# Two shared pools of on-chip buffers in a mixed attention kernel, with the order planned anew

## The chip, the cores and the metric

The kernel runs on one core of one Trainium2 chip. A core has five engines that run side by side, each through its own list of instructions: TensorE (PE, matmuls; PEld is its loading of weights), VectorE (DVE), ScalarE (ACT, here the exponentials), GpSimd (POOL) and SyncE (SP, which here issues nearly all DMAs). They wait for each other by semaphores. The metric is the device time of one launch in microseconds.

## The reference

The input x has 2048 rows of 512 numbers. Two attentions with 32 heads of 16 numbers each work on the same x, and a gate per row mixes them.

```python
x = A_x
g = _sigmoid((x * gate_w).sum(-1, keepdims=True))
a = _A_ref(x, A_wqkv, A_w_phi, A_wo)     # linear attention
b = _B_ref(x, B_wqkv, B_wo)              # full softmax attention
return g * a + (1 - g) * b

# in A, with q, k, v of x @ wqkv per head:
pq = einsum("bhsd,hdf->bhsf", q, w_phi)
phi_q = concatenate([softmax(pq), softmax(-pq)])      # the same for k
kv = einsum("bhsf,bhsd->bhfd", phi_k, v)
z  = einsum("bhsf->bhf", phi_k)
o  = einsum(phi_q, kv) / (einsum(phi_q, z) + 1e-6)     # then @ wo

# in B:
p = softmax(einsum("bhqd,bhkd->bhqk", q, k) * 0.25)
o = einsum("bhqk,bhkd->bhqd", p, v)                    # then @ wo
```

B is the great part of the work: 32 heads of 2048 x 2048 scores, each with an exponential.

## The kernel before

**Work of B.** It is cut into 32 sets. A set has 512 queries (a quarter), a group of 8 heads of which it takes 4, and all 2048 keys as 16 key tiles of 128. For a key tile PE makes the scores of the four heads (L1249, into the seven banks of psR, keys in the partitions and 512 queries along the row), an engine takes exponentials, and PE adds the products with the values into psO (L1300). The exponential of a key tile runs in one of two ways. On ACT it is the exponential function, two instructions of 128 x 1024, each into a buffer of the ring E (L1264). On DVE it is four instructions of 128 x 512 that write 16-bit integers, whose bits are read as a rough bf16 exponential, into a buffer of the ring T (L1269); two copies of it with a small constant added, in two buffers of the ring TS, correct it. Such a shift is one instruction of DVE (L1281) or of POOL (L1284), and the products with these copies use values scaled beforehand (vS). Six of the 16 key tiles of a set may go either way; the rest is for ACT. At the end of a set psO is copied out (OT), turned by a DMA transpose (OTT), divided by its sums (ob, L1211) and, for every pair of sets, turned again into oBT (L1330).

**Work of A.** The maps' weights are first multiplied into the projection: WAT, the turned weights of A, times a block matrix of w_phi gives Wp (L1018). For every 128 rows, `phi` makes one full matmul of x and Wp, two exponentials on ACT (L1077), and the sums of 16 neighbours on POOL in steps: L1083 into a buffer `tr`, L1088, L1089, then L1092 or L1093; POOL then scales the map (L1096 for queries, L1099 for keys). Key maps stay in the ring phk until the 4 tiles of a quarter are multiplied with the values vA (L1122). Query maps are turned by DMA into phT (L1153), multiplied with kz (L1159), divided and gated into oA (L1165), and turned by DMA into oAT (L1169). The gate itself is 64 matmuls of one column in four groups of 16 (L1001), and one matmul of four columns for a certificate on the size of gate_w (L1047). The last projections (L1346, L1358) read oAT and oBT, and 16 tiles of 128 x 512 go out (L1372, L1375).

**Buffers.** In the kernel before each kind has its own ring: 12 of E, 6 of phk, 3 of T, 4 of TS, 2 each of oAT and oBT. xT, W_Av, WAT and Wp are tensors of their own. When weights are no longer needed, their room is used again: the query maps and `tr` lie in WAT, phT and the last outputs in half of Wp, oA and the other outputs in W_Av.

**Order.** The order of each engine's list is made when the program is built, by a planner (`_Sched`). Every operation has an engine, a due time, a length and a delay until its result is there; a DMA transpose has for instance 1.3 us of issue and 2.0 or 2.6 us until it has landed. The planner goes through time and places on each engine the ready operation that can start first, with due times to settle ties, and its own rules for PE (`_pick_pe`) and for which of two ways a key tile takes. An operation that needs a buffer gets one that is free by the planner's times, among several the one with the highest number:

```python
got = sorted(times, key=lambda i: (max(times[i], when), -i))[:len(ts)]
```

The new owner then depends on all operations of the old one (`advance`), and `plan` turns the dependencies that are not implied by others into semaphore waits. The table `STYLES` gives a seed for each stretch of `WINDOW` us of planned time; the seed sets the tolerances of the planner's choices in that stretch (0 stands for the fixed ones).

**The other way out.** A flag computed on the chip says whether the score sizes allow these shortcuts; if not, the same program runs a plain version (`_general`) afterwards. With the inputs given it is skipped.

Of the kernel before, what the change touches and what calls it, by code (L numbers as in the profile page):

```python
# [14 lines left out]
D = 512  # L15
H = 32
DH = 16
# [27 lines left out]
NE_, NPH = 12, 6  # L45
WINDOW = 3.0
STYLES = (
# [478 lines left out]
def _general(fast):  # L526
# [9 lines left out]

    xT, Wp, W_Av, WAT, kz, kvs = ns.xT, ns.Wp, ns.W_Av, ns.WAT, ns.kz, ns.kvs
    T = [x.bitcast(BF16) for x in ns.T_r.aps + ns.TS_r.aps]
# [10 lines left out]
    qst_r, qz_r, oAT_r, oBT_r = sub(ns.qst_r), sub(ns.qz_r), sub(ns.oAT_r), sub(ns.oBT_r)  # L549
# [7 lines left out]
    wat = add("sp", lambda e: e.dma_start_transpose(WAT[:], ns.A_wqkv[:, 0:2 * D]), dma=True)  # L557
    wav = add("sp", lambda e: e.dma_start(W_Av[:], ns.A_wqkv.rearrange("(t p) c -> p t c", p=128)[:, :, 2 * D:3 * D]), dma=True)
    ewp = []
    for w in range(2):  # L560
        for t in range(KT):
            m = _Tile(M_r)

            def fn(e, m=m, w=w, t=t):
                ins = None
                for r in range(KT):
                    ins = e.matmul(m.ap[:, 128 * r:128 * (r + 1)], lhsT=WAT[:, 4 * w + r, 128 * t:128 * (t + 1)],
                                   rhs=ns.Wbd[:, r, :], start=True, stop=True)
                return ins
            f = add("pe", fn, [wat], [m])  # L570
            ewp.append(add("dve", lambda e, m=m, w=w, t=t: e.tensor_copy(Wp[:, w, t, :], m.ap), [f], [m]))
# [9 lines left out]
    def phi(w, st, out):  # L581
        m, mx, d, ee, ss = _Tile(M_r), _Tile(st_r), _Tile(d_r), _Tile(e_r), _Tile(ss_r)
        f = project(m, lambda t: xT[:, t, 128 * st:128 * (st + 1)], lambda t: Wp[:, w, t, :], ewp)
# [16 lines left out]
    for qd in range(4):  # L600
        items = []
        for st in range(4 * qd, 4 * qd + 4):
            ph, va, m = _Tile(phk_r), _Tile(vA_r), _Tile(M_r)
            o = phi(1, st, ph)
            f = project(m, lambda t, st=st: xT[:, t, 128 * st:128 * (st + 1)], lambda t: W_Av[:, t, :], [wav])
# [25 lines left out]
    for qc in range(QC):  # L631
# [32 lines left out]
        for g in range(KT):  # L664
            m, qs, qz = _Tile(M_r), _Tile(qst_r), _Tile(qz_r)
            f = project(m, lambda t, g=g: ns.W_Bq[:, t, 128 * g:128 * (g + 1)], lambda t, qc=qc: xT[:, t, NQ * qc:NQ * (qc + 1)], [])
# [57 lines left out]
def _build(ctx, nc, A_x, A_wqkv, A_w_phi, A_wo, B_wqkv, B_wo, gate_w, out):  # L724
# [58 lines left out]
    wp1 = Wp[:, 1].rearrange("p a b -> p (a b)")  # L783
# [360 lines left out]
    for st in range(NT):  # L1144
# [4 lines left out]
        if st % 4 == 0:  # L1149
            oat[st // 4] = _Tile(oAT_r)  # L1150
# [330 lines left out]
```

## Time and profile before

| | |
|---|---|
| device time, three runs | 697.72, 698.08, 700.85 us; median 698.08 us |
| the profiled execution | 696.97 us |
| span in its profile, first to last instruction | 695.1 us |
| mean granted clock of TensorE in it | 0.990 |
| busy: PE, DVE, ACT, POOL | 656.6, 656.6, 661.1, 525.5 us |

The page of the profile gives busy times, a chain of work followed back from the last instruction, and groups of instructions: line, engine, operation, what is written and read, shapes and type, count, then the busy time in us and the mean time of one in ns, then the idle time of the engine just before them and what ended most of it. A busy time of ACT or DVE is that of the union: neighbours overlap, so one instruction can last longer than the pace at which they follow each other. SPq and ACTq are the queues in which an engine issues DMAs. The granted clock is the share of full speed that TensorE was given. A tile is named by the tensor that it lies in, without its number: "WAT" in a row of POOL is a query map or a `tr` buffer.

### The profile page before, as it was taken

What the parts mean: (1) busy time and instruction counts of PE and PEld (TensorE: products, weight loads), DVE (VectorE), ACT (ScalarE), POOL (GpSimd) and SP (SyncE); (2) the same over time, 40 slices, a digit from 0 to 9 for tenths busy, and PEclk for the clock granted to TensorE, in tenths of its full rate; (3) what the DMA queues carried; (4) which work ended last, traced back from release to release, by engine and by line L of the source; (5) the groups of instructions that cost most, each with busy time, mean ns of one, the idle gap of its engine ahead of it and who ended that gap; (6) DMA issues with size and microseconds to landing.
All of it is one profiled execution on the core that took longest, in us unless ns stands there. A gap on an engine that the chain in (4) does not pass through costs nothing.

```text
span 695.1 us, 16428 instructions
## 1 busy us (share of the span) xinstructions
PE 656.6 (94%) x6760; PEld 213.9 (31%) x6760; DVE 656.6 (94%) x1111; ACT 661.1 (95%) x747; POOL 525.5 (76%) x433
## 2 busy tenths in 40 slices
PE   8999999999999999999998999999899999999996
PEld 4343343332323223233332223232222332222221
DVE  5899979999999999999999999999999999999995
ACT  6999979999999999999999999999999999999992
POOL 6689868887687766777777787778777976777883
PEclk9999989999999999999999999999999999999998
DMA  6501000001000000001022211223221221220001
GB/s 153 152 17 14 19 2 17 16 25 29 11 17 17 9 16 9 17 16 48 16 47 39 40 40 44 47 43 60 24 40 40 52 41 40 38 41 17 16 9 34
DMA packets 72768, 23.81 MB, mean 34 GB/s; under 512 B 64624, under 2 KB 72688, under 8 KB 72688
## 3 DMA queue, kind: packets, MB, share of 16 engines
q1 hardware_dynamic: 71472, 21.93, 15.5%
q8 instruction: 54, 0.88, 0.5%
q10 hardware_dynamic: 1216, 0.79, 0.4%
q14 instruction: 26, 0.21, 0.1%
HBM read 4.21 MB, written 2.10 MB: 9 GB/s over the span
## 4 chain that ended last, share of the span: by engine, by line
ACT 63%; PE 26%; DVE 6%; POOL 2%; DMA 2%; issue 1%; POOLq 0%; DVEq 0%
ACT E L1264 59%; PE psR L1249 9%; PE psO L1300 8%; PE psR L896 4%; DVE T L1269 3%; PE psR L1346 2%; ACT WAT L1077 2%; POOL TS L1284 2%; DMA OTT<-OT 2%; PE psR L958 2%; ACT phk L1077 2%; DVE TS L1281 1%; PE psR L910 1%; DVE ob L1211 0%; DVE OT L879 0%
## 5 line engine op out<-in xcount | busy, mean ns | idle before, releaser
L1264 ACT ACTIVATE E<-psR 128x1024 bf16<-128x1024 f32 x670 | 629.5, 1105 | 14.5 <-PE psR L1249 8.0
L1269 DVE TENSOR_SCALAR T<-psR 128x512 int16<-128x512 f32 x708 | 447.3, 680 | 14.4 <-PE psR L1249 9.6
L1284 POOL TENSOR_TENSOR TS<-T,shc 128x1024 int32<-128x1024 int32 x194 | 364.3, 1891 | 55.9 <-DVE TS L1281 39.7
L1249 PE MATMUL psR<-qz,kT 32*128 32x512 bf16 (+1 forms) x2048 | 292.2, 386 | 28.1 <-ACT E L1264 21.1
L1249 PEld LDWEIGHTS psR<-qz,kT 32*128 32x128 bf16 (+1 forms) x2048 | 77.6, 91 | 274.5 <-ACT E L1264 197.3
L1300 PE MATMUL psO<-TS,vS 128*18 128x512 bf16 x1416 | 125.3, 382 | 2.1 <-POOL TS L1284 1.4
L1300 PE MATMUL psO<-E,vB 128*18 128x512 bf16 x1340 | 122.2, 381 | 0.0
L1281 DVE TENSOR_SCALAR TS<-T 128x2048 int16<-128x2048 int16 x160 | 107.6, 705 | 0.5
L1300 PE MATMUL psO<-T,vB 128*18 128x512 bf16 x708 | 69.2, 381 | 0.0
L1096 POOL TENSOR_TENSOR WAT<-WAT,ss 128x1024 bf16<-128x1024 bf16 x16 | 30.9, 1929 | 26.4 <-DVE TS L1281 24.0
L1300 PEld LDWEIGHTS psO<-TS,vS 128*18 128x18 bf16 x1416 | 30.0, 88 | 57.7 <-issue 31.7
L1099 POOL TENSOR_TENSOR phk<-phk,ss 128x1024 bf16<-128x1024 bf16 x16 | 30.9, 1929 | 22.0 <-DVE TS L1281 21.1
L1300 PEld LDWEIGHTS psO<-E,vB 128*18 128x18 bf16 x1340 | 31.1, 88 | 44.3 <-issue 30.5
L896 PE MATMUL psR<-xT,WB 128*128 128x512 bf16 x128 | 33.7, 388 | 0.1
L896 PE MATMUL psR<-Wp,xT 128*128 128x512 bf16 x128 | 33.2, 382 | 0.6 <-DVE T L1269 0.4
L1083 POOL TENSOR_TENSOR WAT<-phk 128x512 f32<-128x512 bf16 x16 | 18.5, 1154 | 13.3 <-DVE TS L1281 12.6
L1083 POOL TENSOR_TENSOR WAT<-WAT 128x512 f32<-128x512 bf16 x16 | 18.5, 1155 | 12.1 <-DVE TS L1281 11.5
L1088 POOL TENSOR_TENSOR tr<-WAT 128x256 f32<-128x256 f32 x32 | 23.3, 728 | 2.3 <-DVE TS L1281 1.3
L1300 PEld LDWEIGHTS psO<-T,vB 128*18 128x18 bf16 x708 | 17.3, 88 | 20.8 <-issue 17.5
L879 DVE CAST OT<-psO 128x512 bf16<-128x512 f32 x31 | 21.1, 681 | 0.0
L1077 ACT ACTIVATE WAT<-psR 128x512 bf16<-128x512 f32 x32 | 18.9, 697 | 0.0
L1089 POOL TENSOR_TENSOR tr<-tr 128x128 f32<-128x128 f32 x32 | 12.7, 398 | 7.8 <-DVE TS L1281 7.0
(116 smaller groups left out, 362.4 us busy)
## 6 DMA issues: line engine op xcount, KB each, us to landing
qz<-qst SPq DMA_DIRECT2D x120, 16.0 KB, 1.8
out_dram<-WAv SPq DMA_DIRECT2D x12, 128.0 KB, 1.7
WB<-in_B_wqkv_dram SPq DMA_DIRECT2D x3, 384.0 KB, 5.1
T<-in_A_x_dram SPq DMA_DIRECT2D x2, 256.0 KB, 4.4
T<-in_A_x_dram ACTq DMA_DIRECT2D x2, 256.0 KB, 4.8
WAv<-in_A_wqkv_dram SPq DMA_DIRECT2D x1, 512.0 KB, 5.4
WB<-in_B_wo_dram SPq DMA_DIRECT2D x1, 512.0 KB, 3.3
WB<-in_A_wo_dram SPq DMA_DIRECT2D x1, 512.0 KB, 3.6
```

Of the source, the lines that this page charges most:

```text
L896: calls = [lambda e, t=t: e.matmul(tile.ap[:, off:off + 512], lhsT=lhs(t), rhs=rhs(t), start=(t == 0), stop=(t == KT - 1)) for t in range(KT)]
L1077: ex = [add("act", prio, 0.48, lambda e, s=s: e.activation(ev()[:, :, 16 * s:16 * s + 16], P(), ACTF.Exp, scale=1.0 - 2.0 * s), deps=[f] + ...
L1083: p1 = pool(prio + 2, 1.14, lambda e: e.tensor_tensor(v8(), eg()[:, :, 0:8], eg()[:, :, 8:16], ALU.add), ex + use_wat, tiles=[ee, tr], nam ...
L1088: p2 = pool(prio + 2, 0.72, lambda e: e.tensor_tensor(u4(), v8()[:, :, 0:4], v8()[:, :, 4:8], ALU.add), [p1], tiles=[tr, tr2])
L1096: return pool(prio + 6, 1.9, lambda e: e.tensor_tensor(eg(), eg(), ss.ap[:, 0, :].unsqueeze(2).to_broadcast([128, 64, DH]), ALU.mult), p4, ...
L1099: return pool(prio + 6, 1.9, lambda e: e.tensor_tensor(eg(), eg(), ss.ap[:, 1, :].unsqueeze(2).to_broadcast([128, 64, DH]), ALU.mult), [o7 ...
L1249: ins = e.matmul(rs[h].ap, lhsT=kT[a:a + n, g, 128 * kt:128 * (kt + 1)], rhs=qt.ap[a:a + n, c, :], start=True, stop=True, tile_position=(a ...
L1264: exps.append(add("act", pr + 0.5 * cc, 0.905, lambda e, rs=rs, E=E: e.activation(E.ap.rearrange("p (a n) -> p a n", n=512), pair(rs), ACT ...
L1269: exps.append(add("dve", pr + 0.5 * cc + 0.01 * h, 0.6, lambda e, rs=rs, T=T, cc=cc, h=h: e.tensor_scalar(T.ap[:, 1024 * cc + 512 * h:1024 ...
L1281: sh.append([add("dve", pr + 1.0 + 0.3 * m, 0.6, lambda e, T=T, X=X, m=m: e.tensor_single_scalar(X.ap, T.ap, SHIFT[m], ALU.add), deps=exps ...
L1284: sh[-1].append(pool(pr + 1.0 + 0.3 * m, SHP, lambda e, T=T, X=X, m=m: e.tensor_tensor(X.ap.bitcast(I32), T.ap.bitcast(I32), shc[:, m - 1: ...
L1300: ins = e.matmul(O.ap[32 * col:32 * col + VW, :], lhsT=lhs(hd), rhs=rhs(cc)[:, 512 * h:512 * (h + 1)], start=(first_pv[s] == key), stop=(l ...
```

## The change

Nothing of the arithmetic changes. The rings become two pools:

- E has 16 buffers of 128 x 1024 bf16 (256 KB). It holds exponentials of ACT, key maps, query maps, their turned form, `tr`, oA, output tiles and the small scratch of the certificate.
- T has 20 buffers of 128 x 2048 16-bit numbers (512 KB), one tensor. It holds the DVE tiles and both shifted copies, x as staged and the four quarters of the turned x, the two neighbouring halves of WAT, the value weights of A, the second half of Wp, and the maps oAT and oBT.

Every user takes a buffer when the planner places it and gives it back when the last reader is done; the tensors that were reused by hand are gone, and with them the waits for the last use of the old weights (`use_wat`, `use_wav`, `use_wp1`). DMAs that write or read pool buffers (phT, oAT, output) get a semaphore each instead of one per buffer. The order of all engines is planned anew, with a table of seeds for stretches of 2 us in place of 3 us. The plain version loads x again, since its buffers have been reused. Line numbers grow by 6 to 7 in the places named above (L1264 is L1270, L1088 is L1095).

```diff
-NE_, NPH = 12, 6
-WINDOW = 3.0
+NE_, NT_, NPH = 16, 20, 5
+WINDOW = 2.0
 STYLES = (
...
-    xT = sb([128, KT, S], name="xT")
-    W_Av = sb([128, KT, D], name="WAv")
-    WAT = sb([128, 8, D], name="WAT")
-    Wp = sb([128, 2, KT, D], name="Wp")
+    Wp0 = sb([128, KT, D], name="Wp")
...
     E_r = ring(NE_, [128, 1024], name="E")
-    T_r = ring(3, [128, 2048], I16, name="T")
-    TS_r = ring(4, [128, 2048], I16, name="TS")
-    phk_r = ring(NPH, [128, 1024], name="phk")
+    T_all = sb([128, NT_, 2048], I16, name="T")
+    T_r = _Slots([T_all[:, i, :] for i in range(NT_)])
+    TS_r = T_r
+    phk_r = E_r
-    oAT_r = ring(2, [128, KT, NQ], name="oAT")
-    oBT_r = ring(2, [128, KT, NQ], name="oBT")
...
-    watv = WAT[:].rearrange("p a b -> p (a b)")
-    eA_r = _Slots([watv[:, 1024 * i:1024 * (i + 1)] for i in range(2)])
-    tr_r = _Slots([watv[:, 2048 + 1024 * i:3072 + 1024 * i].bitcast(F32) for i in range(2)])
-    phT_r = _Slots([wp1[:, 1024 * i:1024 * (i + 1)].rearrange("p (g q) -> p g q", q=128) for i in range(2)])
-    oA_r = _Slots([W_Av[:, i, :] for i in range(2)])
-    fin_r = _Slots([W_Av[:, 2 + i, :] for i in range(2)])
+    quad = lambda tile: tile.ap.bitcast(BF16).rearrange("p (t n) -> p t n", n=512)
+    xt, wat, wav, wp1 = [_Tile(T_r) for _ in range(QC)], [_Tile(T_r), _Tile(T_r)], _Tile(T_r), _Tile(T_r)
+    wat[0].mate, wat[1].mate = wat[1], wat[0]
...
-    op_wav = dma("sp", -94.5, 8.0, W_Av[:], A_wqkv.rearrange("(t p) c -> p t c", p=128)[:, :, 2 * D:3 * D], deps=op_x23, name="wav")
+    op_wav = dma("sp", -94.5, 8.0, lambda: quad(wav), A_wqkv.rearrange("(t p) c -> p t c", p=128)[:, :, 2 * D:3 * D], deps=op_x23, name="wav", tiles=[wav])
...
     def phi(prio, w, st, ee, ee_deps):
-        tile, ss, tr = _Tile(M_r), _Tile(ss_r), _Tile(tr_r)
+        tile, ss, tr = _Tile(M_r), _Tile(ss_r), _Tile(E_r)
...
-        ph, ptt, rA, oA, nd = _Tile(eA_r), _Tile(phT_r), _Tile(rA_r), _Tile(oA_r), [_Tile(M_r), _Tile(M_r)]
+        ph, ptt, rA, oA, nd = _Tile(E_r), _Tile(E_r), _Tile(rA_r), _Tile(E_r), [_Tile(M_r), _Tile(M_r)]
-            oat[st // 4] = _Tile(oAT_r)
+            oat[st // 4] = _Tile(T_r)
...
-            obt[qc] = _Tile(oBT_r)
+            obt[qc] = _Tile(T_r)
...
-        fi = _Tile(fin_r) if not last else None
+        fi = _Tile(E_r)
```

More of the change, by code (lines that the diff above doesn't have):

```diff
@@ L1000, in gate_mm @@
                 for t in range(KT):
-                    ins = e.matmul(tg.ap[:, st:st + 1], lhsT=xT[:, t, 128 * st:128 * (st + 1)], rhs=gw[:, t:t + 1],
+                    ins = e.matmul(tg.ap[:, st:st + 1], lhsT=XT(t, 128 * st, 128 * (st + 1)), rhs=gw[:, t:t + 1],
                                    start=(t == 0), stop=(t == KT - 1))
             return ins
-        gops.append(add("pe", st_(GT), 0.9, gate_mm, deps=sum(op_x, []) + op_gw, tiles=[tg], mode="full", name="gate", nb=st_(GT - 0.7)))
+        gops.append(add("pe", st_(GT), 0.9, gate_mm, deps=sum(op_x, []) + op_gw, tiles=[tg] + xt, mode="full", name="gate", nb=st_(GT - 0.7)))
     op_ge = add("act", st_(GT), 0.3, lambda e: e.activation(ez[:], tg.ap[:, 0:NT], ACTF.Exp), deps=gops, tiles=[tg])
@@ L1017, in fn, with gram @@
                 for r in range(KT):
-                    ins = e.matmul(tile.ap[:, 128 * r:128 * (r + 1)], lhsT=WAT[:, 4 * w + r, 128 * t:128 * (t + 1)],
+                    ins = e.matmul(tile.ap[:, 128 * r:128 * (r + 1)], lhsT=WAT(4 * w + r, 128 * t, 128 * (t + 1)),
                                    rhs=Wbd[:, r, :], start=True, stop=True)
                 return ins
-            f = add("pe", prio, 0.3, fn, deps=[op_wat] + op_wbd, tiles=[tile], mode="full", name="wp", nb=prio - EARLY)
+            f = add("pe", prio, 0.3, fn, deps=[op_wat] + op_wbd, tiles=[tile] + wat, mode="full", name="wp", nb=prio - EARLY)
             use_wat.append(f)
-            ev_wp[w].append(evac("dve", prio, lambda w=w, t=t: Wp[:, w, t, :], lambda tile=tile: tile.ap, [f], [tile], name="wpev"))
-    def gram(prio, src, deps, name, col):
+            ev_wp[w].append(evac("dve", prio, lambda w=w, t=t: Wp(w, t), lambda tile=tile: tile.ap, [f], [tile] + [wp1] * w, name="wpev"))
+    def gram(prio, src, deps, name, col, also=()):
         m = _Tile(M_r)
@@ L1346, in _build @@
         calls = [lambda e, tile=tile, sl=sl, src=src, w=w, n=n, early=early: e.matmul(
-            tile.ap, lhsT=src.ap[:, n % 4, sl], rhs=w[:, n % 4, :], start=(n == 0), stop=(n == 7 - early))
+            tile.ap, lhsT=quad(src)[:, n % 4, sl], rhs=w[:, n % 4, :], start=(n == 0), stop=(n == 7 - early))
             for n, (src, w) in enumerate(([(oT, WoA)] * KT + [(oBt, WoB)] * KT)[:n_mm])]
-        fi = _Tile(fin_r) if not last else None
+        fi = _Tile(E_r)
         f = chain(prio, calls, MM, [op_oAT[st], op_woA, op_woB] + [x for g in range(KT - last) for x in op_oBT[qc, g]] +
-                  (tail_qk if last and not early else []), [tile, oT, oBt] + ([fi] if fi else []), "of", prio - EARLY, 1 if last else PIECE)
-        dst = (lambda fi=fi: fi.ap) if not last else (lambda i=i: finl[i])
+                  (tail_qk if last and not early else []), [tile, oT, oBt], "of", prio - EARLY, 1 if last else PIECE)
+        dst = lambda fi=fi: fi.ap[:, 0:512]
         if early:
@@ L1358, in _build @@
             f = add("pe", st_(32.0) - 20, MM, lambda e, tile=tile, oBt=oBt, sl=sl, early=early: e.matmul(
-                tile.ap, lhsT=oBt.ap[:, KT - 1, sl], rhs=WoB[:, KT - 1, :], start=early, stop=True),
+                tile.ap, lhsT=quad(oBt)[:, KT - 1, sl], rhs=WoB[:, KT - 1, :], start=early, stop=True),
                 deps=[f, op_oBT[qc, KT - 1][i // 2]], tiles=[tile, oT, oBt], mode="full", name="os")
@@ L1369, in _build @@
                 dst(), tile.ap, omg[:, st:st + 1], None, op0=ALU.mult),
[L1370 removed]
+                deps=[f, op_omg], tiles=[tile, fi], name="fin")
         if not last:
             outs.append(add("sp", prio + 1, 0.63, lambda e, dst=dst, st=st: e.dma_start(out[0, 128 * st:128 * (st + 1), :], dst()),
[L1373 removed]
+                            deps=[ev], tiles=[fi], dma=2.0, name="out"))
         else:
             outs.append(add("act" if i == 3 else "sp", prio + 1, 0.55, lambda e, dst=dst, st=st: e.dma_start(
[L1376 to L1377 removed]
+                out[0, 128 * st:128 * (st + 1), :], dst()), deps=[ev], tiles=[fi], dma=2.6, name="out"))
     op_end = add("sp", 1e9, 0.1, lambda e: None, deps=outs, name="end")
```

106 lines of the change are left out of this document (55 added, 51 removed), and 33 rows, old and new, of the table STYLES.

## The prediction

> **What bounds the kernel now.** I read the page first: the busy times, the chain and the groups.
>
> ```profile
> PE 656.6 (94%) x6760; PEld 213.9 (31%) x6760; DVE 656.6 (94%) x1111; ACT 661.1 (95%) x747; POOL 525.5 (76%) x433
> ...
> ACT 63%; PE 26%; DVE 6%; POOL 2%; DMA 2%; issue 1%; POOLq 0%; DVEq 0%
> ...
> L1264 ACT ACTIVATE E<-psR 128x1024 bf16<-128x1024 f32 x670 | 629.5, 1105 | 14.5 <-PE psR L1249 8.0
> L1269 DVE TENSOR_SCALAR T<-psR 128x512 int16<-128x512 f32 x708 | 447.3, 680 | 14.4 <-PE psR L1249 9.6
> L1284 POOL TENSOR_TENSOR TS<-T,shc 128x1024 int32<-128x1024 int32 x194 | 364.3, 1891 | 55.9 <-DVE TS L1281 39.7
> L1281 DVE TENSOR_SCALAR TS<-T 128x2048 int16<-128x2048 int16 x160 | 107.6, 705 | 0.5
> ```
>
> ACT, DVE and PE are all busy 94 to 95% of 695.1 us, and the chain lies on ACT for 63% and on PE for 26%. All idle time of ACT is 695.1 - 661.1 = 34.0 us; that, and busy time in which its instructions follow each other late (rival D), is all that an order or a pool can win on it. The table by stretches shows where it lies (columns after the length: busy us of PE, PEld, DVE, ACT, POOL, then the granted clock).
>
> ```profile
> 12.00:50.00 38.00, 36.39 (x388) 14.84 (x387) 34.06 (x56) 36.17 (x41) 28.85 (x25) 1.00 0.40 97
> 50.00:100.00 50.00, 48.80 (x568) 19.61 (x567) 45.76 (x77) 43.47 (x48) 41.22 (x30) 0.93 0.08 12
> 100.00:150.00 50.00, 49.15 (x518) 17.54 (x518) 48.41 (x79) 48.17 (x55) 42.11 (x36) 1.00 0.06 12
> 150.00:650.00 500.00, 474.98 (x4887) 146.25 (x4883) 488.26 (x829) 495.80 (x565) 377.66 (x300) 1.00 0.16 32
> 680.00:695.10 15.10, 8.54 (x52) 2.40 (x48) 6.92 (x14) 1.64 (x3) 5.07 (x3) 0.79 0.12 38
> ```
>
> From 150 to 650 us ACT is idle for only 4.2 us. From 12 to 150 us it is idle for 1.83 + 6.53 + 1.83 = 10.2 us, while PE is near full with the projections; behind 680 us it is idle for 13.5. So the places to win are the first 150 us and the tail, and the place to lose is the long middle, where any new wait of ACT goes straight to the end. The waits and the chain give the prices:
>
> ```profile
> ACT oBT L1327 <- PE psR L1320: 8.7, 1, 8.7
> ACT E L1264 <- PE psO L1300: 4.3, 3, 3.8
> PEld psO L1300 <- issue: 79.7, 340, 0.4
> PEld psO L1300 <- POOL TS L1284: 14.2, 45, 1.0
> POOL WAT L1083 <- DVE TS L1281: 24.1, 18, 2.0
> DVE T L1269 <- POOL TS L1284: 0.4, 1, 0.4
> ...
> 67.87 2.40 DVE T L1269 x4
> 181.43 1.19 PE psO L1300 x20
> 605.42 39.96 ACT E L1264 x44
> ```
>
> In the wait rows the numbers are total us, times, longest. An E buffer that PE had not read in time stopped ACT 3 times, for 4.3 us, 3.8 of them at once. From the chain: an exponential on ACT costs 39.96/44 = 0.908 us when nothing is late, one on DVE 2.40/4 = 0.60, a group of four product matmuls into psO 1.19/5 = 0.24. A turn of PE to such products shows 79.7/340 = 0.234 us of idle weight load.
>
> **The change part by part.** Counts here are those of the two built programs' instruction orders, without times.
>
> *Work.* ACT has 668 exponentials instead of 670, DVE 712 instead of 708, DVE shifts 159 instead of 160, POOL shifts 197 instead of 194, PE 8 matmuls into psO more. ACT: -2 x 0.908 = -1.8 us. DVE: 4 x 0.60 less one shift of 0.705, +1.7. POOL: 3 x 1.891 = +5.7, covered by its 695.1 - 525.5 = 169.6 us of idle. PE: 2 groups x 0.24 = +0.5. Over ACT and DVE together the sum is about zero, so the moved tiles alone are no gain; their worth depends on which engine ends last, priced at the tail.
>
> *Turns of PE.* Changes between the three kinds of matmul (32- or 64-row scores, 18-column products, full ones) fall from 1132 to 1112. At 0.234 each that is 4.7 us, less the 0.5 above 4.2; the bounds are 0 (the idle was a wait for another engine) and 4.2. PE carries 26% of the chain, so I take 4.2 x 0.26 = -1.1.
>
> *The stop at 95 to 100 us.* The timeline there:
>
> ```profile
> 94.36 0.61 PE L1249 MATMUL psR<-qz,kT 32*128 32x512 bf16 x3
> 94.90 1.89 PE L958 MATMUL psR<-WB,xT 128*128 128x128 bf16 x16
> 95.01 1.02 ACT L1264 ACTIVATE E<-psR 128x1024 bf16<-128x1024 f32 x1 [0.81 <-PE psR L1249]
> 96.58 0.29 PE L1047 MATMUL psR<-gw,ones 128*128 128x1 bf16 x4
> 96.73 1.75 PE L896 MATMUL psR<-xT,WB 128*128 128x512 bf16 x4
> 98.42 0.40 PE L1249 MATMUL psR<-qz,kT 32*128 32x512 bf16 x4
> 99.83 1.02 ACT L1264 ACTIVATE E<-psR 128x1024 bf16<-128x1024 f32 x1 [3.80 <-PE psO L1300]
> ...
> 92.00:96.00 4.00, 4.00 (x56) 2.62 (x55) 2.52 (x6) 3.19 (x5) 1.89 (x1) 0.50 0.02 4
> 96.00:100.00 4.00, 4.00 (x42) 1.73 (x40) 2.24 (x5) 0.20 (x2) 1.41 (x3) 0.72 0.00 0
> ```
>
> After the four gate groups of 16 one-column matmuls the granted clock is 0.50, and PE takes 98.42 - 94.36 = 4.06 us from one bundle of scores to the next (a V projection, the sum of gw2, a K projection). ACT, whose 12 E buffers are full, also needs the products behind them. In the new order the same four gate groups stand together, but behind them come 6 scores, 16 products, 3 scores, V projection and sum, 5 scores. So the longest gap without scores is 1.89 + 0.29 = 2.18 us at the same low clock. Gain 4.06 - 2.18 = 1.9 us; bounds 0 (the clock stays low for longer) and 0.81 + 3.80 = 4.6 (all of it goes). I take -1.9, the row being of the same work at the same clock.
>
> *Tail.*
>
> ```profile
> 662.95 16.72 ACT L1264 ACTIVATE E<-psR 128x1024 bf16<-128x1024 f32 x18
> 679.46 2.48 DVE L1269 TENSOR_SCALAR T<-psR 128x512 int16<-128x512 f32 x4
> 682.05 1.67 DVE L1281 TENSOR_SCALAR TS<-T 128x2048 int16<-128x2048 int16 x1
> 683.80 1.89 POOL L1284 TENSOR_TENSOR TS<-T,shc 128x1024 int32<-128x1024 int32 x1 [0.63 <-DVE TS L1281]
> 685.75 0.40 PE L1300 MATMUL psO<-TS,vS 128*18 128x512 bf16 x4 [0.51 <-POOL TS L1284]
> ```
>
> ACT's last exponential ends at 679.67; the last DVE tile and its shifts hold the final product until 685.75, 6.1 us later, and ACT sits idle for the 8.7 us of the wait row. In the old order the five product groups behind the last scores are all of DVE tiles. In the new one ten groups follow, four of them of E, and the last but one is an E group: the two engines end together. With the same total work both then end at the middle of 679.67 and 685.75: -3.0 us. Bounds: 0 (they end together because ACT came later) and -6.1.
>
> *Pools.* E, phk, tr, phT, oA, fin and the exponentialed maps share 16 buffers of 256 KB (before 12 + 6, with the rest in dead weights); T, TS, input, weights and output maps share 20 of 512 KB, 4 of them held by the input for most of the run. The slack is not what the counts suggest: exponentials of ACT that must wait for a product's read are 26 before and 21 after, of DVE 29 and 34, so the planner uses the room up to the edge again. DVE tiles that wait for a POOL shift's buffer fall from 72 to 22; the row above shows that this cost 0.4 us: gain at most 0.4, taken as 0.
>
> *New waits.* 45 exponentials of ACT now wait for something that is neither PE nor ACT: 21 for POOL (the second step of a sum, L1088 before, which sets a tr buffer free), 24 for a DMA's landing (12 oAT, 8 output, 4 phT). Behind a waiting exponential stands everything else of ACT, then PE's scores, which wait for its psR banks. The DMAs:
>
> ```profile
> oAT<-WAv SPq DMA_TRANSPOSE x16, 2.4
> out_dram<-WAv SPq DMA_DIRECT2D x12, 128.0 KB, 1.7
> Wp<-WAT SPq DMA_TRANSPOSE x16, 3.2
> WAT<-in_A_wqkv_dram SPq DMA_TRANSPOSE x1, 6.0
> ...
> 23.41 3.85 SPq L834 DMA_TRANSPOSE WAT<-in_A_wqkv_dram  x1
> ...
> L1018 PE MATMUL psR<-Wbd,WAT x32: 219/220/315, 61.1 to 94.1; 128*128 128x128 bf16 x32
> ```
>
> The planner's own entries allow 1.3 + 2.0 = 3.3 us for oAT, 2.63 for an output, 3.9 for phT; the rows (2.4, 1.7, 3.2) are shorter, so I take 0 for these 24; if a queue ahead on SP made each late by as much as the margin plus 0.5 us, 12 us. For POOL there is no such margin: PE waits for POOL's shifts 184 times after and 183 before, and 45 of those before cost 14.2/45 = 0.32 us. At that rate 21 x 45/183 = 5 waits cost 0.32: +1.6 us; bounds 0 and 21 x 1.0 (the longest) = 21. Separate wait instructions rise on ACT from 1 to 47 and fall on DVE from 124 to 70; DVE keeps its 0.60 pace with 124 of them, so 0. On SP the load of A's value weights now waits for a POOL shift and a product before it goes out; behind it stand the WAT transpose and then the q spreads. WAT landed at 23.4 + 6.0 = 29.4 us and is first read at 61.1, so 31 us of lateness are covered there. The q spreads behind it feed the scores of the second head group; a wait for one early shift holds them by 1.9 us at most (one shift, L1284). I take 0. The 242 DMAs themselves are the same in number and size.
>
> Sum: -1.1 - 1.9 - 3.0 + 1.6 = -4.4 us. The profiled execution took 696.97 (1.87 outside its span of 695.1) and lies 1.1 under the median 698.08; against the first that is 692.6, on the median's footing **693.7 us**.
>
> **The rivals.**
>
> *A: POOL holds ACT (slower).* The waits for tr buffers sit behind POOL's own waits for DVE shifts: the row of L1083, the step ahead of it, has 18 such waits of 24.1/18 = 1.34 us. If the 21 waits of ACT cost 0.5 us each (half the longest that PE shows), they cost 10.5 and the sum is -6.0 + 10.5 = +4.5: 702.6. It is slower by over 0.5% from 9.5/21 = 0.45 us each. Against it: PE's mean over all 183 waits is 0.08.
>
> [...]
>
> *B: the pools do not bind.* ACT's waits for buffers were 4.3 us in all, one event, and three engines at 94 to 95% leave nothing else: gains and waits cancel, 697 to 698.5. For it: the unchanged 26 against 21 waits on products. Against: the tail's order is plainly another.
>
> *C: the low clock comes again.* In the new order 29 scores stand around the gate groups between one product and the next (before 20), so PE's thin stretch is longer. If the stop stays and a second one of 4.6 us follows: -4.4 + 1.9 + 4.6 = +2.1: 700.2, within the bound.
>
> [...]
>
> *D: all of PE's lateness shrinks.* At 0.908 each, 670 exponentials would take 608 us; the page has 629.5, so 21 us are stretch from late scores. A third of it gone besides: 693.7 - 7 = 686.7.
>
> **How the numbers follow.** A measurement of this kernel tells about 0.5% (3.5 us) from no change: faster is below 694.6, slower above 701.6. My forecast holds 0.36, D 0.16, B 0.12, C 0.10, A 0.26. Faster 0.52, same 0.22, slower 0.26. The forecast's own range is 690 (tail at twice its size) to 697. The range over the cases goes from 685, under D, to 704, over A's 702.6; what is left out is A at over 0.55 us a wait and an even better D.
>
> **What would show it.** Right: no ACT wait of over 2.5 us near the gate; ACT's last wait ahead of its final copy (8.7) at 3 to 6 us; ACT's waits for POOL of about 1.6 us in sum and for DMAs near 0; ACT idle from 150 to 650 us still under 7 us. Wrong: rows of ACT waiting for POOL L1095 above 6 us in sum (A), a second stretch with a clock of 0.50 (C), the middle's ACT idle unchanged but its busy time down by several us (D), or a wait of SP near 20 us that holds the q spreads.

## The result, and the profile after

| | before | after |
|---|---|---|
| median | 698.08 us (697.72 to 700.85) | **692.74 us** (688.26 to 693.53, 4 executions) |
| the profiled execution | 696.97, span 695.1, clock 0.990 | 693.2, span 691.4, clock 0.985 |

The ratio is 0.9889, with a 95% interval of 0.9847 to 0.9932. The new kernel is faster by 1.1%; the forecast was 693.7 us. More executions of both (run new_again, below) gave 690.91 against 698.27 us, ratio 0.9882 (0.9847 to 0.9917).

The page after: busy times, the line of granted clock in 40 slices, the chain, and the groups that answer to those shown of before.

```profile
PE 642.8 (93%) x6706; PEld 212.7 (31%) x6768; DVE 659.0 (95%) x1114; ACT 659.1 (95%) x745; POOL 530.7 (77%) x436
...
PEclk8999989999999999999999999999999999999998
...
ACT 52%; PE 30%; DVE 11%; issue 3%; DMA 1%; POOL 1%; DVEq 0%; ACTq 0%; POOLq 0%
...
L1270 ACT ACTIVATE E<-psR 128x1024 bf16<-128x1024 f32 x668 | 627.6, 1093 | 16.7 <-PE psR L1255 15.0
L1275 DVE TENSOR_SCALAR T<-psR 128x512 int16<-128x512 f32 x712 | 448.5, 678 | 10.0 <-PE psR L1255 7.9
L1290 POOL TENSOR_TENSOR T<-T,shc 128x1024 int32<-128x1024 int32 x197 | 370.1, 1891 | 65.7 <-DVE T L1287 38.2
...
L1287 DVE TENSOR_SCALAR T<-T 128x2048 int16<-128x2048 int16 x159 | 107.8, 714 | 0.5 <-PE psO L1306 0.4
```

ACT accounts for the span: 2.0 us less work (two exponentials fewer), and 1.7 us less idle (34.0 to 32.3). The waits show that this 1.7 is a difference of larger numbers:

```profile
PEld psO L1306 <- issue: 84.5, 352, 0.8
POOL E L1106 <- DVE T L1287: 19.3, 9, 3.7
...
ACT E L1270 <- PE psR L1255: 15.0, 36, 1.7
POOL E L1090 <- DVE T L1287: 11.6, 9, 1.8
...
PEld psO L1306 <- POOL T L1290: 9.2, 29, 1.0
...
DVE T L1275 <- PE psR L1255: 7.9, 23, 0.8
...
ACT T L1333 <- PE psR L1326: 3.4, 1, 3.4
```

ACT's wait ahead of its last copies fell from 8.7 to 3.4 us (-5.3). Its idle time before exponentials rose from 14.5 to 16.7 us (+2.2): behind late scores it rose by 7.0, from 8.0 to 15.0, while the 4.3 us behind products (psO, which hold E buffers) are gone. What is left, +1.4, lies in the main behind ACT's last work, in the issue and the landing of the outputs. -2.0 - 5.3 + 2.2 + 1.4 = -3.7, the difference of the spans. There is no row of ACT waiting for POOL at all, and none for psO.

Where scores are later shows in the stretches (columns as before: PE, PEld, DVE, ACT, POOL, then the granted clock). The first fence answers to the rows shown of before; the second has the places of half clock in the new kernel, the third the same three in the kernel before.

```profile
12.00:50.00 38.00, 36.18 (x371) 14.74 (x373) 33.43 (x54) 34.75 (x39) 30.95 (x25) 0.91 0.40 99
50.00:100.00 50.00, 46.94 (x551) 19.25 (x553) 47.34 (x76) 45.12 (x49) 44.71 (x31) 0.94 0.06 12
100.00:150.00 50.00, 47.84 (x524) 17.94 (x532) 47.90 (x80) 47.69 (x54) 39.81 (x37) 0.99 0.06 12
150.00:650.00 500.00, 469.05 (x4885) 146.11 (x4926) 492.19 (x839) 494.73 (x563) 386.34 (x303) 1.00 0.17 32
680.00:691.40 11.40, 4.58 (x36) 1.96 (x35) 3.70 (x10) 1.64 (x3) 0.00 (x0) 0.84 0.16 51
```

```profile
12.00:18.80 6.80, 6.22 (x35) 2.77 (x34) 4.53 (x8) 5.14 (x6) 4.37 (x4) 0.50 0.81 200
94.00:100.70 6.70, 6.61 (x54) 2.85 (x52) 5.76 (x11) 3.84 (x6) 4.54 (x5) 0.50 0.01 2
647.00:650.20 3.20, 3.20 (x30) 0.60 (x27) 2.16 (x4) 2.46 (x3) 3.20 (x2) 0.50 0.21 41
```

```profile
12.00:18.80 6.80, 6.03 (x64) 3.08 (x63) 4.68 (x8) 6.61 (x9) 5.66 (x5) 1.00 0.83 185
94.00:100.70 6.70, 6.70 (x69) 3.80 (x68) 3.74 (x8) 2.09 (x4) 2.28 (x4) 0.68 0.01 2
647.00:650.20 3.20, 2.46 (x25) 0.68 (x22) 3.02 (x6) 3.20 (x5) 3.20 (x3) 1.00 0.21 41
```

In its profiled execution the new kernel ran at half clock at 12 to 19 and at 647 to 650 us too, where the old one had the full clock. In these two stretches ACT did 5.14 and 2.46 us of work instead of 6.61 and 3.20. At the gate it lost less than before: ACT and DVE together were busy for 9.60 us there instead of 5.83. ACT is idle for 5.3 us from 150 to 650 us (4.2 before) and for 10.4 from 12 to 150 (10.2 before); what grew there is DVE's work, 492.19 us in the middle instead of 488.26.

The end of the new kernel, as a timeline: start, length, engine, line and what is done.

```profile
677.73 2.01 ACT L1270 ACTIVATE E<-psR 128x1024 bf16<-128x1024 f32 x2
...
677.90 1.89 POOL L1290 TENSOR_TENSOR T<-T,shc 128x1024 int32<-128x1024 int32 x1
...
678.20 2.14 DVE L1287 TENSOR_SCALAR T<-T 128x2048 int16<-128x2048 int16 x1 [0.44 <-PE psO L1306]
...
680.40 0.39 PE L1306 MATMUL psO<-T,vS 128*18 128x512 bf16 x4
...
684.54 2.36 SPq L1381 DMA_DIRECT2D out_dram<-E  x3
```

ACT's last exponential ends at 679.74 (before 679.67), the last product starts at 680.40 (before 685.75). The two engines do end together. But of the 5.35 us only 3.7 reach the span's end: the products come before most of the last projections, which filled the wait before, and SP took 2.36 us to issue the last three outputs, 1.48 before. That issue is no cost of the new order: with the same end of the program it took 2.75 us in the trace of extra_two_places and 1.32 in that of extra_gate_too.

### The profile page after: what moved, and what is told of

The parts are those of the page before. It is cut to its first block, busy times and chain, and to the rows that moved or that the text cites. A ratio compares the mean times of both kernels' runs of the same rounds, so it can differ in the third digit from the quotient of the medians.

```text
span 691.4 us, 16395 instructions
## 1 busy us (share of the span) xinstructions
PE 642.8 (93%) x6706; PEld 212.7 (31%) x6768; DVE 659.0 (95%) x1114; ACT 659.1 (95%) x745; POOL 530.7 (77%) x436
## 4 chain that ended last, share of the span: by engine, by line
ACT 52%; PE 30%; DVE 11%; issue 3%; DMA 1%; POOL 1%; DVEq 0%; ACTq 0%; POOLq 0%
ACT E L1270 50%; PE psR L1255 11%; PE psO L1306 9%; DVE T L1275 6%; PE psR L902 4%; DVE T L1287 3%; ACT E L1084 3%; PE psR L1352 2%; PE psR L964 2%; POOL T L1290 1%; DMA E<-E 1%; DMA out_dram<-E 1%; PE psR L916 1%; DVE ob L1217 0%; DVE OT L885 0%
## 5 line engine op out<-in xcount | busy, mean ns | idle before, releaser
L1270 ACT ACTIVATE E<-psR 128x1024 bf16<-128x1024 f32 x668 | 627.6, 1093 | 16.7 <-PE psR L1255 15.0
L1290 POOL TENSOR_TENSOR T<-T,shc 128x1024 int32<-128x1024 int32 x197 | 370.1, 1891 | 65.7 <-DVE T L1287 38.2
L1306 PE MATMUL psO<-T,vS 128*18 128x512 bf16 x1424 | 128.3, 384 | 1.3 <-POOL T L1290 1.0
L1287 DVE TENSOR_SCALAR T<-T 128x2048 int16<-128x2048 int16 x159 | 107.8, 714 | 0.5 <-PE psO L1306 0.4
L1306 PEld LDWEIGHTS psO<-T,vS 128*18 128x18 bf16 x1424 | 30.7, 88 | 58.7 <-issue 36.6
L1090 POOL TENSOR_TENSOR E<-E 128x512 f32<-128x512 bf16 x32 | 36.9, 1154 | 14.4 <-DVE T L1287 11.6
L1106 POOL TENSOR_TENSOR E<-E,ss 128x1024 bf16<-128x1024 bf16 x16 | 30.8, 1928 | 19.3 <-DVE T L1287 19.3
L1103 POOL TENSOR_TENSOR E<-E,ss 128x1024 bf16<-128x1024 bf16 x16 | 30.8, 1928 | 18.5 <-DVE T L1287 18.3
L1084 ACT ACTIVATE E<-psR 128x512 bf16<-128x512 f32 x64 | 37.5, 680 | 0.0
L902 PE MATMUL psR<-T,WB 128*128 128x512 bf16 x106 | 28.9, 387 | 3.8 <-issue 3.2
L902 PE MATMUL psR<-T 128*128 128x512 bf16 x111 | 29.5, 381 | 3.0 <-issue 1.6
L1352 PE MATMUL psR<-WB,T 128*128 128x512 bf16 x113 | 30.1, 381 | 2.3 <-DVE T L1275 0.9
L1095 POOL TENSOR_TENSOR tr<-E 128x256 f32<-128x256 f32 x32 | 23.3, 728 | 3.1 <-DVE T L1287 2.6
```

The source lines that it names most:

```text
L902: calls = [lambda e, t=t: e.matmul(tile.ap[:, off:off + 512], lhsT=lhs(t), rhs=rhs(t), start=(t == 0), stop=(t == KT - 1)) for t in range(KT)]
L1084: ex = [add("act", prio, 0.48, lambda e, s=s: e.activation(ev()[:, :, 16 * s:16 * s + 16], P(), ACTF.Exp, scale=1.0 - 2.0 * s), deps=[f] + ...
L1090: p1 = pool(prio + 2, 1.14, lambda e: e.tensor_tensor(v8(), eg()[:, :, 0:8], eg()[:, :, 8:16], ALU.add), ex, tiles=[ee, tr], name="ps1")
L1103: return pool(prio + 6, 1.9, lambda e: e.tensor_tensor(eg(), eg(), ss.ap[:, 0, :].unsqueeze(2).to_broadcast([128, 64, DH]), ALU.mult), p4, ...
L1106: return pool(prio + 6, 1.9, lambda e: e.tensor_tensor(eg(), eg(), ss.ap[:, 1, :].unsqueeze(2).to_broadcast([128, 64, DH]), ALU.mult), [o7 ...
L1270: exps.append(add("act", pr + 0.5 * cc, 0.905, lambda e, rs=rs, E=E: e.activation(E.ap.rearrange("p (a n) -> p a n", n=512), pair(rs), ACT ...
```

## The experiments

Where an order is kept or edited by hand, one helper does it: in place of `sch.run()`, `replay` places the operations of a written list in that list's order, on their engines, and gives each the buffer that is free first, with the kernel's own rules.

```diff
-    sch.run()
+    sch.replay(ORDER)
...
+    def replay(self, order):
+        self.begin()
...
+                    w, where = self._place(o, self.free[o.eng] if o.half is None or self.last_mode != "row" else
...
+            self.put(o, w, where)
```

Both kernels also have a filler (`fill`), which puts groups of zero-weight product matmuls where the planned times leave PE thin. Under `replay` these times differ a little, and so does their number: 8 groups in pools_only, 10 in one_e_less and 4 in tail_moved, where the two kernels and two_t_less have 3. At 0.24 us each the added ones are 1.2, 1.7 and 0.2 us of PE's time.

**The pools without the new order (pools_only).** The new kernel with `ORDER` taken from the plan of the kernel before.

> The two pools of the new kernel with the order of the kernel before: every engine issues its operations in the order of the kernel before, only the buffers come from the pools. If the pools alone are the gain (my forecast priced them at 0, rival B says that they don't bind): against 698 us, a gain from the pools alone would show as 693 to 695; B expects 697 to 699. Theory now: neither. 16 buffers are fewer than the 12 + 6 and the six reused ones of before, so an order made for the rings stalls ACT for buffers while the maps are made (100 to 300 us): 700 to 704, with waits of ACT's exponentials on PE's products or POOL that before has not.

Measured: 701.67 us (698.43 to 704.72), ratio to before 1.0044 (1.0016 to 1.0072). The pools make the old order slower by 3 us, also at the same granted clock (0.993: 699.1 to 699.6 us, before 695.9 to 697.1). The profile shows one place of it, 200 to 250 us, where key maps are summed; the first fence is the kernel before, the second this run:

```profile
200.00:250.00 50.00, 47.59 (x475) 13.87 (x473) 48.75 (x84) 50.00 (x59) 37.20 (x31) 1.00 0.06 12
```

```profile
200.00:250.00 50.00, 44.99 (x461) 13.60 (x462) 46.95 (x79) 47.38 (x56) 35.93 (x30) 1.00 0.06 12
```

ACT loses 2.62 and DVE 1.80 us there. Four of the filler's groups lie at 218.7 to 245 us, so not all of that is shown to be the buffers' doing. At 216 to 219 us ACT waits for a buffer, once for a product and once for POOL's second step of a sum, the mechanism of rival A:

```profile
216.39 1.02 ACT L1576 ACTIVATE E<-psR 128x1024 bf16<-128x1024 f32 x1 [0.55 <-PE psO L1612]
...
218.68 1.94 ACT L1576 ACTIVATE E<-psR 128x1024 bf16<-128x1024 f32 x2 [0.78 <-POOL tr L1401]
```

These two waits are all that ACT has for a buffer in this trace. The greater part of its added idle time is behind late scores, 12.6 us instead of 8.0; how that follows from the buffers is not shown.

**The pools and the rings with the same other seeds (rings_other_seeds, pools_other_seeds).** Both kernels planned anew with one table of 360 entries drawn at random.

```diff
-WINDOW = 3.0
-STYLES = (
-    0, 0, 0, 885634, 162398, 933473, 485575, 0, 0, 0, 0, 0, 797800, 31386, 686204, 297615, 979543, 369985, 746347, 924778,
...
+WINDOW = 2.0
+STYLES = (570666, 960438, 656116, 635018, 878150, 577540, 751985, 877094, 416426, 157933, 158988, 0, 777259, 814990, 795063,
...
```

> The kernel before, planned with another table of seeds (drawn at random, windows of 2 us), its buffers the rings as before. It is the partner of the next run, which has the same seeds and the pools. Expected far above 698 us (730 to 770), since this table was not searched.

> The new kernel, planned with the same random table as the run before it. If shared pools by themselves let the planner keep the engines busy, it is 8 us or more under that run; if the gain of the change comes from the searched table alone, the two lie within 4 us of each other, on either side.

Measured: 757.6 us with rings, 747.5 with pools. With this table the order planned for the pools is 10.1 us better than the one planned for the rings, though the pools cost 3 under the old order. It is one draw: how far two draws lie apart on the same buffers was not measured, so the 10.1 is not shown to be the pools' doing. The traces point both ways. ACT's exponentials wait 24.4 us for products where the rings had 38.7, and 38.7 us for scores where the rings had 25.7. What is clear is that the searched table is worth more than that: 747.5 - 691 = 56 us against this draw.

**Which pool is full (one_e_less, two_t_less).** The new kernel's own order, with fewer buffers handed out.

```diff
-        for i, ten in enumerate(slots.tenant):
+        for i, ten in list(enumerate(slots.tenant))[:getattr(slots, "cap", None)]:
...
-    sch.run()
+    E_r.cap, T_r.cap = 15, 20
+    sch.replay(ORDER)
```

> The new kernel's order on every engine, with 15 of the 16 buffers of E in use (T keeps 20). If the pool E is used up to its edge, ACT waits for products or other readers where it had a buffer before: 3 to 12 us more than the new kernel (694 to 704), with waits of ACT's exponentials on psO, DMA or POOL. If the pools don't bind, as rival B has it, the time stays at 690 to 693.

> The new kernel's order on every engine, with 18 of the 20 buffers of T in use (E keeps 16), 1 MB less. By the waits of the profile after (no exponential of DVE waits for a buffer) T has room: 690 to 693, as the new kernel. If T binds too: 694 or more, with waits of DVE's exponentials on POOL or psO.

Measured: 701.27 us with one buffer of 256 KB less, ratio to before 1.0033 (1.0011 to 1.0055), and 692.96 with two of 512 KB less, 0.9905 (0.9871 to 0.9939). The first loses the whole gain. The second loses about 1 us at most: at a clock of 0.993 it took 689.1 us, the new kernel 688.3 and 688.4. As it keeps the order by the same helper, it also shows that the helper does not cost the 9 us of the first. In the waits of the first, a row stands that the new kernel has not:

```profile
ACT E L1576 <- PE psO L1612: 11.3, 16, 1.9
```

ACT waited 16 times for a product to give an E buffer back. So E is used to its last buffer, and T has at least two, 1 MB, that this order hardly needs.

**The tail alone (tail_moved).** The kernel before, with its order edited in the last set. In the list the first column is the operation, the second its engine.

```diff
-qk31.13 x4     pe
-expd31.13 x4   dve
-sh31.13        dve
-shp31.13       pool
-pv31.13 x3     pe
-shp31.9        pool
+qk31.13 x2     pe
+exp31.13 x2    act
+pv31.13        pe
+sh31.9         dve
```

> The kernel before with only its end changed: key tile 13 of the last set goes to ACT instead of DVE, as in the new kernel, one shift of key tile 9 goes from POOL to DVE, and the product groups that wait for them move in PE's list. If the tail is the gain, as the term of -3.0 (0 to -6.1) says, the time falls from 698 to 694 to 696, the last exponential of ACT ends 1.8 us later and the last product 2 to 4 us earlier. If the tail is covered by something else, for instance the output projections, it stays at 697.5 to 699.

Measured: 695.44 us, ratio 0.9956 (0.9931 to 0.998), that is -3.1 us (-4.8 to -1.4). ACT's last wait is 3.6 us instead of 8.7, and its last exponential ends at 681.2 instead of 679.7:

```profile
ACT oBT L1637 <- PE psR L1630: 3.6, 1, 3.6
```

```profile
678.26 2.96 ACT L1574 ACTIVATE E<-psR 128x1024 bf16<-128x1024 f32 x3
...
679.75 1.89 POOL L1594 TENSOR_TENSOR TS<-T,shc 128x1024 int32<-128x1024 int32 x1 [2.91 <-DVE TS L1591]
...
682.13 0.39 PE L1610 MATMUL psO<-E,vB 128*18 128x512 bf16 x4
```

With one key tile moved from DVE to ACT the last product starts at 682.13, 3.6 us earlier, so the term of the tail is shown alone, without pools. Its size is less sure than the median has it, for the two sets of executions differ in clock: seven of the twelve here had 0.996, two of the 59 of the kernel before. At 0.996 they took 694.1 to 695.5 us (median 694.9); the seven of the kernel before at 0.995 and 0.996 took 695.9 to 697.2 (median 696.4), which is 1.4 us more. The two profiled executions lie 2.2 us apart (694.8 and 696.97). There, two more exponentials at 0.908 would end ACT 1.8 us later and it ended 1.55 later, so about 0.25 of the 2.2 goes with the clock. The tile is thus worth 1.4 to 2 us at a like clock and 3.1 by the medians.

**The half clock (extra_two_places, extra_first_place, extra_gate_too, before_extra_gate).** Added matmuls that keep PE at work ahead of the stretches of half clock. Each is a group of four product matmuls with zero weights, as the kernels already place three times; they add zero to psO.

```diff
     sch.fill(idle, narrow, last_pv, set_O)
+    extra = {895: 2, 898: 1, 899: 2, 1067: 1, 1070: 2, 6012: 1, 6013: 2, 6115: 2}
+    s = 0
+    for o in list(sch.order["pe"]):
+        s = o.run[0] if o.kind == "pv" else s
+        for k in range(extra.get(o.seq, 0)):
+            x = idle(o, set_O[s])
+            x.start = x.end = o.start + 0.0001 * (k + 1)
+            sch.order["pe"].insert(sch.order["pe"].index(o) + 1 + k, x)
```

In this table the first five entries lie at 9 to 14 us; the last three make 5 groups at 642 to 646 us (13 in all, not the 14 that the expectation says). extra_first_place has the first five entries alone; extra_gate_too has also `330: 2, 331: 2, 332: 2, 333: 2`, the gate groups, and before_extra_gate these four alone.

> The new kernel with 14 added groups of product matmuls with zero weights (they add zero): 8 in PE's gaps at 9 to 14 us, 6 at 642 to 646 us, ahead of the two stretches of half clock (12 to 19 and 647 to 650 us) that the kernel before does not show. If those stretches cost as rival C says (they come from a thin PE), the granted clock stays at 1 there and the time falls from 692.7 to 687 to 690. If the half clock there is covered by PE's idle time, the time stays at 692 to 693.5, or rises by up to 14 x 0.24 = 3.4 us if PE is what the others wait for.

> The new kernel with the 8 added groups of zero weights at 9 to 14 us alone. The two places together gave 691 to 693 less 689.4. If the cost lies in the half clock at 12 to 19 us, this run gives 689 to 690 with a clock of 0.993 or, where the stretch at 647 us comes, 0.990; if it lies at 647 us, it stays at 691 to 692.

> As the run before, and two more such groups behind each of the four gate groups (8 in all), ahead of the half clock at 94 to 101 us. If the stop there costs what the kernel before shows (4.6 us at most, 3.0 by ACT's gaps of 1.46 and 1.54 us in the new one), another 1 to 3 us less than the run before; if the added matmuls themselves (8 x 0.24 and turns, about 2.7 us) cost PE, which is full there, as much as the clock gives back, no difference within 1 us.

> The kernel before with two groups of product matmuls with zero weights (they add zero) behind each of its four gate groups. If the stop at 95 to 100 us is the half clock's, 1 to 4.6 us less than 698 us at 0.995 or more of clock; if the added matmuls (8 x 0.24 us and turns, 2.7 us) cost what the clock gives back, as in the new kernel, 697 to 699 us.

> The new kernel unchanged, for more executions beside those of the kernel before on one chip. The kernel before took 695.9 to 703.0 us with a mean granted clock from 0.996 to 0.982, about 0.5 us for each 0.001. If the half clock in the new kernel is a matter of chance in each execution, as there, its executions lie on such a line too: about 688 us where the clock is 0.993, 693 to 694 where it is 0.985, and at the same clock 7 to 9 us under the kernel before. If the stretches at 12 and 647 us belong to its order, nearly all executions have them: 692 to 694 at 0.985 to 0.988.

| run | executions | median us | lowest, highest | mean granted clock |
|---|---|---|---|---|
| the kernel before, beside all runs | 59 | 698.2 | 695.89, 702.96 | 0.982 to 0.996 |
| the new kernel, the first 4 and new_again | 10 | 691.8 | 687.36, 693.53 | 0.985 to 0.994 |
| extra_first_place | 6 | 689.96 | 688.32, 691.02 | 0.990 to 0.996 |
| extra_two_places | 6 | **689.39** | 688.57, 689.89 | 0.993 to 0.994 |
| extra_gate_too | 6 | 688.95 | 688.5, 690.06 | 0.998 to 1.000 |
| before_extra_gate | 12 | 697.45 | 696.17, 699.26 | 0.992 to 0.998 |

The stretches of the run with both places:

```profile
12.00:18.80 6.80, 6.64 (x79) 3.30 (x81) 5.18 (x9) 6.40 (x8) 4.75 (x5) 1.00 0.55 116
94.00:100.70 6.70, 6.54 (x76) 2.70 (x69) 5.87 (x12) 4.95 (x7) 3.35 (x5) 0.83 0.01 2
647.00:650.20 3.20, 3.20 (x37) 0.84 (x35) 3.20 (x7) 3.20 (x5) 1.85 (x1) 1.00 0.20 41
```

And its page, busy times and the two groups of exponentials, with the last row of ACT's exponentials in its timeline:

```profile
PE 640.6 (93%) x6758; PEld 211.9 (31%) x6820; DVE 658.3 (96%) x1114; ACT 658.7 (96%) x745; POOL 530.6 (77%) x436
...
L1270 ACT ACTIVATE E<-psR 128x1024 bf16<-128x1024 f32 x668 | 627.3, 1093 | 12.6 <-PE psR L1255 11.4
L1275 DVE TENSOR_SCALAR T<-psR 128x512 int16<-128x512 f32 x712 | 448.3, 677 | 7.7 <-PE psR L1255 5.5
```

```profile
671.07 3.81 ACT L1270 ACTIVATE E<-psR 128x1024 bf16<-128x1024 f32 x4
```

The full clock is back at the first and third place, and ACT's work there with it (6.40 and 3.20 us). The median is 689.39, ratio to before 0.9851 (0.9818 to 0.9885), 2.4 us under the new kernel's, and all six executions are faster than seven of the new kernel's ten. How large the gain over the new kernel is stays unsure, since the intervals of the two ratios overlap. What the groups do is make the good case the usual one: all six had a clock of 0.993 or 0.994, of the new kernel's ten only three, and those three (687.4 to 688.4 us) were faster by about 1 us, which may be the groups' price. extra_first_place alone has 689.96 us and 0.993 in four of six, as was expected if the cost lies at the first place. The third place is not shown to need its groups: in the profile of new_again the clock from 600 to 650 us is 1.00 without them (0.97 in the first profile of the new kernel).

At the gate the same remedy brings nothing: the clock rises to 0.998 and the time moves by 0.4 us; in the kernel before the ratio is 0.9992 (0.9974 to 1.001), and its six executions at 0.997 and 0.998 (696.2 to 697.4 us) are no faster than the kernel before at 0.993 to 0.996 (695.9 to 697.2). That the added matmuls take there what the clock gives fits this, but was not separated from a half clock that costs little at this place.

new_again came out between its two expectations: four of its six executions had 0.987 to 0.990 and took 690.2 to 692.7 us, two had 0.993 and 0.994 and took 688.4 and 687.4. The half clock comes in most executions of the new kernel, not in all.

The executions show what goes with the half clock. Each pair is a mean granted clock and the times at it:

```
kernel before   0.993: 695.9 to 697.1 (8)    0.988: 698.2 to 701.3 (8)    0.982: 702.1 to 703.0 (3)
new kernel      0.993: 688.3, 688.4          0.988: 692.3                 0.985: 693.2, 693.5
```

The spread of both kernels, 6 to 7 us, goes with the clock. At one clock, 0.993, the new kernel is 8 us under the old; the two profiled executions, at 0.985 and 0.990, show only 3.8 of it. The mean clock also counts the half clock at the end of the trace, which has another length in each (688.74 to 695.10 us in the profile before, 687.83 to 691.40 after), and the half clock at the gate, whose removal brought 0.4 us above, so this comparison is good to a microsecond or two.

## Why the prediction was right, and where it was not

The time was right (693.7 against 692.74), and so was the sign. Its parts came out as follows:

- **Work, 0: the pieces right, the balance wrong.** ACT's busy time fell by 2.0 us (1.8 forecast) and DVE's rose by 2.4 (1.7). But DVE fitted its added work into a shorter span: its idle time fell from 695.1 - 656.6 = 38.5 to 691.4 - 659.0 = 32.4 us. The sum had no term for that.
- **Tail, -3.0: the mechanism right, the size not settled.** I took the middle of 679.67 and 685.75. Measured in the trace are -5.3 on ACT's last wait and -3.7 at the span's end, behind projections that had filled the wait and a longer issue of the last outputs. I had subtracted nothing for that work. tail_moved shows 1.4 to 2 us for the tile alone at a like clock, 3.1 by the medians.
- **New waits of ACT on POOL, +1.6: wrong, 0.** The trace has none. The step that failed took PE's rate of late shifts (0.32 us for a quarter of them) for ACT's waits on another kind of buffer. The planner hands a buffer out only where its last reader is done by its own times, which may be why; that was not tested. Rival A (702.6, chance 0.26) falls with it. Its mechanism exists: with the old order on the pools ACT waited 0.78 us for such a step. That SP's and the DMAs' part was 0 held but for 0.3 us before one exponential (an output's landing). POOL's waits for DVE shifts are there in the new trace too (19.3 us in 9 waits, 11.6 in 9): the planner itself makes each POOL operation wait, by semaphore, for the DVE shift placed before it (`o.deps.append(self.sh[-1])`). ACT feels none of these waits.
- **The stop at the gate, -1.9: borne out by the busy sums.** From 50 to 100 us ACT and DVE together were busy for 45.76 + 43.47 = 89.23 us before and 47.34 + 45.12 = 92.46 after, 1.6 us more for each. ACT's idle gaps there, in this timeline of the new kernel, are 1.34 and 1.42 us, under the 2.5 that I named:

```profile
97.56 1.02 ACT L1270 ACTIVATE E<-psR 128x1024 bf16<-128x1024 f32 x1 [1.34 <-PE psR L1255]
100.01 1.97 ACT L1270 ACTIVATE E<-psR 128x1024 bf16<-128x1024 f32 x2 [1.42 <-PE psR L1255]
```

- **Turns of PE, -1.1: not shown.** The row by which I priced them, PEld's idle time by issue before products, rose from 79.7 (340 times) to 84.5 us (352).
- **Pools, 0: half right.** I read the room as used up to the edge and gave the pools no price. E is at the edge (one buffer less costs 9 us), T is not; and under the old order they cost 3 us. The order planned for the pools was 10 us better under the same seeds, in one draw. In the new kernel the exponentials' waits for products, which give the buffers back, are gone: ACT's had been 4.3 us (3.8 of it at the gate), and DVE's are in this row of the kernel before:

```profile
DVE T L1269 <- PE psO L1300: 1.6, 5, 0.4
```

The new trace has no such row of either engine; ACT has one wait for a buffer left, the 0.3 us above. DVE's idle time ahead of exponentials falls from 14.4 to 10.0 us, and to 7.7 with the added matmuls. What of this the pools did and what the new order did is not shown.
- **Rival C had the cost right, and the place and reason wrong.** Its sign came, further stretches with a clock of 0.50, but at 12 and 647 us. At the gate, where it put the second stop, the new kernel lost less than the old one. That a thin stretch of PE would bring one there was an assumption; PE was busy for 3.14 of the 3.41 us ahead of the half clock at the gate. Its 4.6 us is the right size: the trace with the clock restored ends its last exponential at 671.07 + 3.81 = 674.88 us, 4.9 before the new kernel's. But such stretches come and go with the execution in both kernels, so it was no rival to the tail and the order but a cost beside them. 700.2 was too high, since the sum it was added to was too small.
- **Rival D's time, 686.7, is near the new kernel's executions at 0.993 and 0.994 (687.4 to 688.4), by another way.** The pace did not change: 627.6 us for 668 exponentials is 0.940 each, 629.5 for 670 was the same. Rival B (697 to 698.5) falls by the result.

So the total came out in part by luck, since two errors partly cancelled. At equal clock the gain is about 8 us where I had 4.4. But half clock takes more from the new kernel, whose median of 691.8 us lies 3.5 above its executions at 0.993, than from the old one, whose 698.2 lies 1.8 above the median of its own (696.4). That leaves 6.4 us between the medians of all executions, and 5.3 between those of the first ones.

How the 8 us divide can only be told in part. By the trace with the clock restored (span 686.7 at a clock of 0.993, 8.4 under the old one at 0.990): ACT's work 2.4 less, its last wait 5.3 less, its idle time before exponentials 1.9 less, and 1.2 more at the rest. What share of the middle is owed to the pools and what to the searched table stays open: the old order on the pools and the random table on both kernels are the only hints, and the new order on the old rings was not run.

## What to carry to other kernels

When a change replaces an order, compare two traces at the same granted clock, or compare many executions by their clock, before naming causes: here one profile each would have shown less than half of the gain (3.8 of 8 us). Shared buffers made an order slower by 3 us that was not planned for them; run the old order on the new buffers once, and take one buffer away from each pool, to see which size counts. Where PE has gaps ahead of a place at which others wait for it, try a few matmuls of zeros in them: ahead of 12 us, where PE was busy for 2.17 of 3.41 us, 8 groups of four gave a median of 689.96 us instead of 691.8, with a clock from 12 to 50 us of 1.00 instead of 0.91 in the profiles. At the gate, where PE was busy for 6.54 of 6.70 us, 8 more moved the time by 0.4 us.

## What the runs showed of the hardware

In the profile of the new kernel the half clock came after stretches in which PE was busy for most of the time. These are the 3.41 us ahead of three of its starts (at 11.99, 93.91 and 646.87 us), all at full clock:

```profile
8.58:11.99 3.41, 2.17 (x19) 0.70 (x17) 3.41 (x10) 3.16 (x5) 0.35 (x3) 1.00 0.65 107
90.50:93.91 3.41, 3.14 (x52) 1.66 (x48) 3.18 (x6) 3.41 (x4) 3.41 (x3) 1.00 0.00 0
643.46:646.87 3.41, 2.30 (x25) 0.61 (x21) 3.41 (x7) 3.41 (x5) 3.41 (x3) 1.00 0.00 0
```

PE was busy for 2.17, 3.14 and 2.30 of 3.41 us, the second time with the one-column matmuls of three gate groups and scores of 32 rows. In the profile of the kernel before, PE was busy for 3.20 of the 3.41 us ahead of the half clock at the gate (88.00 to 91.41 us), and for only 2.40 of 3.41 us from 499.20 to 502.61, where the clock stayed full, then and after (1.00 from 502.61 to 506.02). So PE's busy time in these stretches does not tell which of them a half clock followed; what does was not shown. Added matmuls with zero weights changed the clock: with the groups added, all six executions of extra_gate_too had a mean clock of 0.998 or more (the ten of the new kernel 0.985 to 0.994), and its profile has 1.00 at the gate, where that of extra_two_places has 0.83.

But for those at the end of the trace, the stretches of half clock in the first profiles of the two kernels last 6.83 us (from 91.41 before, from 11.99 and 93.91 after) or 3.41 us (from 646.87 after). They move: the first one of the new kernel starts at 11.99 us in the first profile and at about 14 in that of new_again (0.64 over 12.00 to 18.80 us, 0.50 over 14.00 to 20.00), and before_extra_gate, whose order is that of the kernel before at this place, has one where the profile of the kernel before had none:

```profile
14.00:20.00 6.00, 5.39 (x33) 3.15 (x35) 2.44 (x4) 4.34 (x6) 4.98 (x5) 0.50 0.71 200
```

So these stretches are not bound to one order.
